# New order lists for all five engines of a fused attention and FFN kernel, with TensorE's identity products as entries of the list

## The chip, the cores and the metric

The kernel runs on one core of a Trainium2 chip. The metric is the device time of one execution in microseconds (us). Before the change it is 241.96 us, the median of three runs (241.48 to 242.43). Five engines work side by side: TensorE (PE in the profile; PEld are its weight loads), VectorE (DVE), ScalarE (ACT), GpSimd (POOL) and SyncE (SP, which here only issues transfers). Each works its own instructions strictly in the order in which they stand, and waits at an instruction until the semaphores of its inputs have been raised.

## The reference

Four batches of eight heads, 768 positions of 64 values. A small 8x8 matrix per head is normalised five times over rows and columns and mixes the eight blocks of 96 positions of K and V. Attention is then local: block i of Q against block i of the mixed K and V. Its output, 3072 tokens of 512 values, goes through an FFN with a leaky rectifier whose slope differs by column.

```python
k_sorted = np.einsum('bhij,bhjcd->bhicd', P, k_b).reshape(B, H, S, D)
v_sorted = np.einsum('bhij,bhjcd->bhicd', P, v_b).reshape(B, H, S, D)
...
scores = scale * np.matmul(q_b, k_sb.transpose(0, 1, 2, 4, 3))
scores = scores - np.max(scores, axis=-1, keepdims=True)
attn = np.exp(scores)
attn = attn / (np.sum(attn, axis=-1, keepdims=True) + 1e-09)
return np.matmul(attn, v_sb).reshape(B, H, S, D).astype(np.float32)
...
h = x @ w_in
g = np.maximum(h, 0.0) + alpha * np.minimum(h, 0.0)
return (g @ w_out).astype(np.float32)
```

## The kernel before

**Stages.** Each batch's K, V and Q are loaded, mixed and laid out, and then attention and the FFN run through the tokens, with the next batch's preparation between them. A *group* g is one block of one batch: g0 to g7 are batch 0, g8 to g15 batch 1, up to g31. A *chunk* c is what one round of the FFN's first product takes: c0 is g0 and g1, c1 is g2 and g3 (192 tokens each), c2 to c8 are four groups each (384 tokens). An *output tile* t is 128 tokens, t0 to t23.

- *K and V of batches 1 to 3.* POOL copies the loaded K (`KS`) into a zero-padded layout `KSz` (`conv_k`, line 672), and V (`VST`) into `VDz` (`conv_v`, line 715; all copies that either engine can make are recorded at line 428, the helper `copy`). Eight products with a mixing matrix (`BDM` or `BDV`) turn a part into PSUM (lines 685 and 726), and ScalarE or VectorE copies it on to `KT` or `VS` (line 428). `KSz` has three places and `VDz` four, so a copy waits until TensorE has read the part that stood there. `conv_v` of batch 0 goes from `VST` into a free part of `hT`, its products are at line 731.
- *Q of batches 1 to 3.* POOL issues eight transfers into `QN` (line 457), then SP issues six transposing transfers `QN` to `QTz` (line 465).
- *Attention of a group.* Scores (lines 769 and 772) into `psS`, their maximum on VectorE (line 778). In batch 0 the scores are computed a second time, turned, with the maximum subtracted (lines 784 and 793), and ScalarE takes the exponential (`ET`, line 816). From batch 1 on ScalarE takes eight exponentials (`Esb`, line 805), and SP issues a transposing transfer `Esb` to `ET` (line 810). Then come the products with V (line 825, `psO`), the reciprocal of the sums (line 833), the scaled result `xq` (line 836), its transposition on TensorE (line 851) or, from batch 2 on, by SP (line 844), and the copy to `xT` (line 428).
- *FFN.* For each of 16 parts of a chunk four products with `w_in` (line 875) into one of two banks `psH` (for c0 also the bank `psP`), ScalarE's rectified copy `t` (line 885) and VectorE's result `hT` (line 888). The bank is free when VectorE is done. An output tile is four quarters of four products with `w_out` each (line 914), a copy to one of four stages `outstg` (line 428) and a store that SP issues (line 928). `hT` holds two chunks of 384 tokens.

**Order.** Nothing is scheduled on the chip. The program adds operations with their inputs and outputs to a graph, numbered 0 to 1225 in the order in which the code adds them. The table `SEQ` lists these numbers in one order for all engines, and `arrange` walks it: each entry goes to the end of its engine's list. Where an operation can run on several engines, a letter says which: `a` ScalarE, `d` VectorE, `p` POOL; without one it is the first of those named in the code. `emit` then writes each list out with the waits that the graph asks for. The planned durations in the graph matter for the entries' start times in the plan, which `fill` and `idle` read.

**Identity products.** `warm` makes products of the identity matrix with 512 columns (line 1041), whose result nobody reads. `fill` puts them into the planned gaps of TensorE's list ahead of the first `w_in` product and of the first `w_out` product; `idle` puts them into planned gaps of 300 ns and more after that, in a bank that is free. There are 55: 15, 8, 2, 2, 4, 2, 5, 5, 1 and 3 ahead of the first `w_in` product, and 1, 1, 1, 2, 1, 1 and 1 behind it.

Of the kernel before, what the change touches and what calls it, by code (L numbers as in the profile page):

```python
# [7 lines left out]
AP = bass.AP  # L8
# [24 lines left out]
0 2 11 3 7 4 8 1 22 9 14 42 28 43 44 19 45 46 5 47 18 48 49 15 50 51 39 52 53 6 54 55 56 25 57 58 29 59 60 61  # L33
23 62 63 12 64 65 66 132 89 37 67 83 68 81 31 69 84 70 32 87 71 13 10 91 88 85 72 40 73 74 90 130 75 76 86 41
77 133 78 82 79 131 92 80 93 134 138 102 94d 103a 26 104 147 95 105a 100 148 98 96d 97 108 99a 38 101d 109d
158 159 118 106a 119d 107a 35 114 160 149 36 115d 116 16 120 117a 112a 146 150 111 110d 113d 161 30 17 122 27
135 123a 24 121a 128 144 124 129d 126 143 125a 151 127d 21 145 136 152 137 162 153 163 164 154 183 155 165
166a 34 156 184 20 157a 167 141 192 33 185 168 193 140 169 194 142 186 170 201 195 139 247 246 249 248 253 252
171 202 198 196 203 204 199 197 187 219 200 220 205 216 213 217 214 218 206 221 215 228 207 188 225 189 222
272 226 229 227 223 230 234 224 260 235 237 236 261 190 262 250 191a 238 269 208 309 270 231 251a 209 239 174  # L40
210 402 401 232 233 240 211 257 254 271 263 212d 255a 290 256 310d 278 264 258 291 273 346 259a 265 266 304
312d 292 279 267 280 303 241 268 293 284 242 281 243 301 282 337 347a 283 274 300 338 302a 244 299 287 245d
285 339 286 311 351d 294 340 313 295 305 296 275 314 288 315 289 319 276a 177 297 306d 316 320 321 307 317 378
298a 318 178 325 308a 379 322 341 323 348 342 182 380 326 324 354 349a 327 328 343 352 180 329 331 353d 381
344 350 345d 356 179 332 330 382 357a 334 383 333 372 335 181 359a 336 360 384 363 361 387 364 362 418 393 403
388a 385 365 366 419 369 358 367 373 370 368 420 374 386d 355d 428 371 394d 391 421 429 434 390d 444 431 392a
435 389 395 432 375 430 436 446 396d 452 445 376d 397 433 404 449 453 437 398a 454 464 447 458 465 399 459 455
474 176 400a 460 405 448 175 456 173 450 466 406 478 451d 422 457 475 476 482 172 423 467 504 424 461 483 494
484 505 462 425 407 477a 463 414 495 426a 480 485 572 573 408a 481d 438 409 486 548 412 439 496 487 508 506
277 440 491 479 417 534 410 411 509 413 416 535 415 507d 441 488 492 497 442d 524 493 489 510 490 515 511a 377  # L50
525 512 516 549 517 513 526 514 468 536 518 537d 521 469 470 519 527 560 520 538 471 561 539a 542 522 472d 571
543 523 498 540 562 550 499 570 500 541d 501 545 544 502a 563 574 546 554 575d 596 547 555 605 557 556 606a
611 503 578 558 576 551 559 579 427 612 580 581 552a 597 584 577 582 533 590 583 585 598 586 528 443 587 529
530 609 613 636 531 599 614 625 532d 608 591 610a 626 588 569 607 592 589 627 637 564 615 616 473 565 634 566
619 635a 628 567 617 638 568d 593 639a 618 620 640 622 641a 621 645 600 594a 676 643 601 658 623 595 677 642
661 659 624 644 678 662 602 663 660 670 679 703 671 603 704 664 604a 647 667 705 665d 648 629 666 691 630 631
692 713 672 668 706 669 712 738 685 739 715 673 686 693 714 687 674 740 675 632 716 633d 688 717 718 697 719d
752 689 741 767 698 690 680 751 749 699 700 553 649 750d 720 701 646 694 702 721 777 722 723 695a 768 753 696
726 780 754a 681 732 682 724 748 727 725 683 733 769 747 728 734 707 729 708 770 709 755 730 742 731 756 778
710 802 779a 812 757 758 782 776 759 761 760 781 735 762 783a 763 657 764 803 736a 813 651 784 814d 849 787  # L60
785 743 765 786 788 653 804 744 654 789 766 745 852 771 793 772 773 805 846 815 794 837 796 816a 795 811 774
790 797 656 798 817 799 853 818a 791d 819 800 838 650 825 820 847 801 839 826 821 655 822 848 806 850 840 807
831 808 652 851a 872 832 883 827 792 823 833 880 824 854 881a 886 834 855 828 856 835 836 884 860 910 885a
829d 857 861 873 882 711 866 858 862 874 887 867 859 911 908 863 909d 888 875 864 841 865 889 900 912 684 890
891 913a 842 901 894 892 746 868 893 902 869 843 844 876 870d 914 897 895 877 896 919 903 898 915d 916 878 934
917 920 879 935 980 918 936 809 981 899 928 775 925 929 904 830 930 926 921 927 960 737 931 961 922 932 937
905 962 906 942 933 982 907 945 923a 963 986 946 948 987 943 949 944 988 938 950 939 940 954 947 989 1006 955
957 1007 810 983 958 1008 959 951 956 971 952d 964 968 972 1009 984a 973 1017 969 965 845 1032 970 977 966 974
941 978 990 979 975 1018 985 976 997 1033 994 924 998 1019 999 995 967 996 1003 991 1000 1004 1020 1005 1001
1034 1002 1023 992 1014 993 1010 1046 1011 1015 1012 1024 1047 1035 1016 1058 1025 1026 871 1059 1029 1027  # L70
1013 1048 1028 1030 1060 1031 1040 1021d 1043 1078 1041 1061 1036 1044 1079 1037 1042 1022 1084 1045 1052 1085
953 1049 1053 1086 1054 1080 1038 1055 1050d 1066 1056 1087 1062 1067 1115 1063 1068 1104 1057 1072 1064 1069
1105 1065 1116 1070 1071 1106 1117 1075 1088 1118 1076 1107 1089 1073 1077 1081 1074 1039 1095 1090 1082a 1092
1096 1051 1136 1097 1093 1119a 1094 1101 1091 1108 1102 1098 1120 1103 1137 1099 1109 1100 1121 1083 1110 1112
1122 1111 1160 1123 1113 1114 1127 1124 1128 1138 1129 1125 1126 1133 1130 1134 1161 1135 1131 1132 1145 1142
1146 1162 1147 1143 1144 1139 1148 1163 1149 1140a 1150 1151 1141 1154 1152 1181 1153 1155 1156 1157 1166 1158
1202 1159 1167 1168 1182 1172 1169 1173 1208 1174 1170 1171 1178 1175 1179 1183 1180 1176 1177 1190 1187 1191
1184 1192 1188 1189 1196 1185a 1193 1186 1197 1209 1198 1194 1195 1210 1164d 1199 1165 1203 1200 1201 1204
1220 1211 1205 1212d 1221 1213 1206d 1222 1223 1207 1214 1224 1215 1216 1225 1217 1218 1219
# [41 lines left out]
class _Graph:  # L121
# [79 lines left out]
    def arrange(self, table):  # L201
        assert len(table) == len(self.ops)
        letters = {"p": "pool", "a": "act", "d": "dve"}
        free = dict.fromkeys(ENGS, 0.0)
        free["pool"] = 400.0
        loads = [0.0, 0.0, {"n": 2, "mark": 193, "usable": 0.0, "end": 0.0, "fills": True}]
        self.order = {e: [] for e in ENGS}
        done = set()
        for x in table:
            op = self.ops[int(x.rstrip("pad"))]  # L210
            e = letters.get(x[-1], op.engs[0])
            assert e in op.engs and op.deps <= done
            done.add(op.idx)
            at = max(free[e], self.ready_at(op, e))
            op.eng, op.start, op.pos = e, at, len(self.order[e])
            free[e], op.end = self.span(op, e, at, free, loads)
            self.order[e].append(op)
        return max(op.end for op in self.ops)

    def fill(self, make, unit, first, spans):  # L220

        out, last = [], self.ops[first].end + 300
        for op in self.order["pe"]:
            for lo, hi in spans:
                begin = max(last, lo)
                n = int((op.start - begin) * 0.9 / unit)
                if op.start <= hi and n > 0:
                    x = _Op("pe", lambda e, n=n: make(e, n), n * unit, 0.0, None, len(self.ops))
                    x.start, x.end, x.banks = begin, begin + n * unit, set()
                    x.deps.add(first)  # L230
                    self.ops.append(x)
                    out.append(x)
            out.append(op)
            last = max(last, op.end)
        for pos, op in enumerate(out):
            op.pos = pos
        self.order["pe"] = out

    def idle(self, make, unit, banks, lo, hi, least):

        used = {k: sorted((op for op in self.ops if k in op.banks), key=lambda o: o.start) for k in banks}
        out, last = [], 0.0
        for op in self.order["pe"]:
            n = int((op.start - last) * 0.85 / unit)
# [841 lines left out]
```

## Time and profile before

| | us |
|---|---|
| median of three runs | 241.96 |
| profiled execution | 242.12 |
| its span, from the first to the last instruction | 240.1 |
| TensorE busy, with the identity products | 231.3 |
| VectorE busy | 172.4 |
| ScalarE busy | 153.9 |
| POOL busy | 99.8 |
| granted TensorE clock, as a share of full speed | 1.0 |

The rows of the profile are to be read so: a group of instructions gives line, engine, operation, what it writes and reads and in which shape, the count, and behind the bar the busy time, the mean duration in ns, the idle time of the engine ahead of them, and what ended that idle time. The timeline and the chain of waits give the start in the span, the duration and what ran. The chain is followed back from the last instruction, at each step to what released it. Matmuls are pipelined and the profile models their ends, so that the duration of a short group is longer than the distance to the next start. SP's and POOL's issues of transfers have a duration of their own, and a time to landing.

### The profile page before, as it was taken

The numbers are of one execution on the slowest core, as the hardware profiler recorded it, in microseconds if no ns is written. First come the engines' busy times: TensorE is split into PE (matmuls) and PEld (weight loads), VectorE is DVE, ScalarE is ACT, GpSimd is POOL, SyncE is SP. The second block draws the span as 40 slices with busy tenths as digits, with TensorE's granted clock in tenths as the row PEclk, the third lists the DMA queues.
The fourth block names the chain that finished last, engine by engine and source line by source line (L and its number), as shares of the span: only waits on it lengthen the run. The fifth ranks groups of instructions, "written<-read, shape, count | busy, mean of one in ns | idle before, by whom it ended". The sixth has DMA issues, their size and how long they took to land.

```text
span 240.1 us, 6229 instructions
## 1 busy us (share of the span) xinstructions
PE 231.3 (96%) x2519; PEld 142.3 (59%) x2519; DVE 172.4 (72%) x348; ACT 153.9 (64%) x422; POOL 99.8 (42%) x146
## 2 busy tenths in 40 slices
PE   7889998999999999999999999999999999999995
PEld 3446676688566656655666566555655555555554
DVE  4756887998989888777958677756777666645542
ACT  4576466678978788977667778567756655444510
POOL 7989707924689964518859841000000000000000
PEclk9999999999999999999999999999999999999999
DMA  5999999999967999999749974593745426101023
GB/s 101 205 211 217 155 220 197 176 180 166 161 118 141 144 128 163 161 180 164 153 101 69 114 137 79 111 183 64 141 121 112 123 49 177 39 0 44 0 91 131
DMA packets 71981, 31.36 MB, mean 131 GB/s; under 512 B 64512, under 2 KB 67344, under 8 KB 71952
## 3 DMA queue, kind: packets, MB, share of 16 engines
q0 software_dynamic: 23408, 13.63, 42.6%
q1 hardware_dynamic: 48544, 17.33, 35.2%
q8 instruction: 20, 0.33, 0.6%
q14 instruction: 9, 0.07, 0.1%
HBM read 27.28 MB, written 6.29 MB: 140 GB/s over the span
## 4 chain that ended last, share of the span: by engine, by line
PE 71%; POOL 11%; DMA 10%; DVE 5%; issue 1%; ACT 0%; POOLq 0%
PE psH L875 29%; PE psYP L914 27%; DMA KS<-in_k_dram 10%; POOL VDz L428 5%; PE psS L914 4%; PE psO L825 3%; PE psS L769 3%; PE psYP L726 2%; PE psYP L685 2%; DVE hT L888 1%; POOL KSz L672 1%; POOL w_in_bf L959 1%; POOL VDz L512 1%; DVE VDz L428 1%; PE psO L914 1%
## 5 line engine op out<-in xcount | busy, mean ns | idle before, releaser
L875 PE MATMUL psH<-xT,w_in_bf 128*128 128x384 bf16 (+1 forms) x556 | 98.4, 311 | 0.6 <-DVE hT L888 0.4
L888 DVE SCALAR_TENSOR_TENSOR hT<-t,omaT,psH 128x384 bf16<-128x384 f32 (+1 forms) x139 | 77.7, 571 | 29.2 <-ACT t L885 27.5
L885 ACT ACTIVATE t<-psH 128x384 f32<-128x384 f32 (+1 forms) x139 | 62.7, 461 | 50.5 <-PE psH L875 49.2
L914 PE MATMUL psYP<-w_out_bf,hT 128*128 128x512 bf16 x336 | 82.9, 379 | 0.0
L875 PEld LDWEIGHTS psH<-xT,w_in_bf 128*128 128x128 bf16 x556 | 49.0, 98 | 29.2 <-DVE hT L888 4.1
L914 PEld LDWEIGHTS psYP<-w_out_bf,hT 128*128 128x128 bf16 x336 | 31.1, 98 | 30.3 <-DVE outstg L428 0.6
L805 ACT ACTIVATE Esb<-psS,nf 96x96 bf16<-96x96 f32 x192 | 46.2, 344 | 2.0 <-DVE nf L778 1.8
L428 POOL COPY VDz<-VST 64x384 bf16<-64x384 bf16 x40 | 34.1, 853 | 15.6 <-PE psYP L726 12.8
L672 POOL COPY KSz<-KS 64x512 bf16<-64x512 bf16 x36 | 22.0, 612 | 18.8 <-PE psYP L685 8.8
L778 DVE TENSOR_REDUCE nf<-psS 96x8 f32<-96x768 f32 x24 | 22.8, 948 | 5.5 <-PE psS L769 5.1
L836 DVE TENSOR_TENSOR xq<-psO,rec 96x512 bf16<-96x512 f32 x31 | 21.2, 683 | 0.6
L457 POOL DMA_DIRECT2D QN<-in_q_dram x24 | 19.9, 837 | 0.3 <-POOL QN L517 0.3
L1041 PE MATMUL psYP<-identb 128*128 128x512 bf16 x51 | 15.1, 417 | 0.7 <-ACT identb L428 0.7
L825 PEld LDWEIGHTS psO<-VS,ET 112*128 112x128 bf16 x248 | 11.3, 98 | 4.7 <-DVE xT L428 0.7
L769 PEld LDWEIGHTS psS<-KT,QTz 128*96 128x96 bf16 x192 | 11.9, 125 | 2.5
L833 DVE RECIPROCAL rec<-psO 96x8 f32<-96x8 f32 x31 | 6.2, 200 | 9.8 <-PE psO L825 9.8
L825 PE MATMUL psO<-VS,ET 112*128 112x65 bf16 x248 | 12.7, 194 | 0.4 <-DVE xT L428 0.3
L769 PE MATMUL psS<-KT,QTz 128*96 128x96 bf16 x192 | 12.6, 209 | 0.0
L428 ACT ACTIVATE VS<-psYP 112x512 bf16<-112x512 f32 x15 | 10.3, 686 | 3.1 <-PE psYP L726 2.6
L428 ACT ACTIVATE KT<-psYP 128x512 bf16<-128x512 f32 x15 | 8.9, 596 | 3.8 <-PE psYP L685 2.5
L726 PEld LDWEIGHTS psYP<-BDV,VDz 128*128 128x128 bf16 x192 | 8.0, 98 | 3.6 <-POOL VDz L428 0.8
L726 PE MATMUL psYP<-BDV,VDz 128*128 128x64 bf16 x192 | 9.6, 193 | 0.5 <-POOL VDz L428 0.5
(142 smaller groups left out, 204.0 us busy)
## 6 DMA issues: line engine op xcount, KB each, us to landing
out_dram<-outstg SPq DMA_DIRECT2D x23, 256.0 KB, 2.6
KS<-in_k_dram POOLq DMA_DIRECT2D x3, 768.0 KB, 8.7
QN<-in_q_dram POOLq DMA_DIRECT2D x24, 96.0 KB, 3.8
w_in_bf<-in_moe_w_in_dram POOLq DMA_DIRECT2D x4, 512.0 KB, 11.9
w_out_bf<-in_moe_w_out_dram POOLq DMA_DIRECT2D x2, 1024.0 KB, 23.3
VST<-in_v_dram POOLq DMA_DIRECT2D x4, 384.0 KB, 18.3
hT<-in_q_dram POOLq DMA_DIRECT2D x1, 768.0 KB, 7.0
VST<-in_v_dram POOLq DMA_DIRECT2D x1, 768.0 KB, 10.9
```

The source lines that it names most:

```text
L428: return e.activation(o, i, ACTF.Copy) if e is nc.scalar else e.tensor_copy(o, i)
L672: G.add(POOL, lambda e, hp=hp: e.tensor_copy(AP(KSz, hp * 64 * 3072 + u % 3 * 1024 + hp * 64, [[3072, 64], [128, 8], [1, 64]]), AP(KS[n], ...
L726: inst = e.matmul(AP(t, off + dd * 64, [[row, 128], [1, 64]]), AP(VDz, (u % VSL * 8 + dd) * 128, [[VSL * 1024, 128], [1, 128]]), AP(BDV, b ...
L769: inst = e.matmul(o, AP(QTz[n], hp * 3072 + h4 * 768 + i * 96, [[6144, 128], [1, 96]]), AP(KT[n], (h4 * 8 + i) * bk, [[ld, 128], [64, 2], ...
L778: G.add(DVE, lambda e: e.tensor_reduce(AP(nx, 0, [[8, 96], [4, 2], [1, 4]]), AP(psX, 0, [[1024, 96], [512, 2], [96, 4], [1, 96]]), AxisLis ...
L805: inst = e.activation(AP(Esb[me], p * 128, [[1024, 96], [64, 2], [1, 48]]), AP(psX, (p // 4) * 512 + (p % 4) * 96, [[1024, 96], [48, 2], [ ...
L825: inst = e.matmul(AP(psZ, hp * 512 + h4 * 68, [[1024, 128], [1, 65]]), AP(ET[me] if far else ET[m], pos(h4, hp) * 96, [[800, nk], [1, 128] ...
L836: G.add(DVE, lambda e: e.tensor_tensor(out=AP(xq[me], 0, [[512, 96], [256, 2], [64, 4], [1, 64]]), in0=AP(psZ, 0, [[1024, 96], [512, 2], [ ...
L875: inst = e.matmul(AP(pt, poff, [[1024, 128], [1, n]]), AP(w_in_bf, kt * DFF + ft * 128, [[KT_TILES * DFF, 128], [1, 128]]), AP(xT, kt * XR ...
L885: G.add(ACT, lambda e: e.activation(AP(t1[tb], 0, [[384, 128], [1, n]]), AP(pt, poff, [[1024, 128], [1, n]]), ACTF.Relu, scale=-1.0), t_ac ...
L888: G.add(DVE, lambda e: e.scalar_tensor_tensor(out=AP(hT, ft * RING + tok % RING, [[FT_TILES * RING, 128], [1, n]]), in0=AP(t1[tb], 0, [[38 ...
L914: inst = e.matmul(AP(bank[0], bank[1], [[1024, 128], [1, n]]), AP(hT, ft * RING + tok % RING, [[FT_TILES * RING, 128], [1, 128]]), AP(w_ou ...
```

## The change

The table is another one; it was searched anew from batch 0's k on. The code outside it changes in these points.

- The identity products are entries of the table, such as `i3Y`: three products into bank `Y`. `filler` adds them when `arrange` comes to them, behind the identity matrix and behind the readers of what last stood in that bank. `fill` and `idle` are gone. There are 46 products in 11 entries: 15, 8, 2, 2, 4, 1, 3, 3, 3, 3 and 2, all ahead of the first `w_in` product.
- Three kinds of operations may run on more engines: the copies of batch 0's Q, `conv_v` of batch 0 and the padding of `KT`. Q's copies and the padding stay where they were.
- 45 copies change their engine: 20 go from ScalarE to VectorE, 20 from VectorE to ScalarE, and three to and two from POOL (all five are `conv_v` of batch 0).

What changes in the order, where the prediction speaks of it:

- POOL: of batch 0's `conv_v` it takes parts 0, 4 and 7 (before: 2 and 5). The load of batch 2's V is issued ahead of the first `KSz` copy. The eight issues of batch 2's Q (line 457) stand behind all sixteen V copies of batch 2; they stood among the last of them.
- VectorE: g0's `xT` copy stands behind g2's maximum. The maxima of g3 to g7 stand ahead of more of c0's and c1's `hT` results. The two `VDz` copies that stood ahead of and behind g5's maximum go to ScalarE and to a place behind g6's `xq`.
- TensorE: c0's first product stands behind g2's second scores. The third quarter of t1 stands behind c2's first product, the product of V part 4 of batch 1 ahead of it.
- SP: the stores of t1 and t0 stand ahead of g8's transposition of `Esb`; they stood behind g10's and g11's. Three of the six transpositions of batch 1's Q stand behind it; all six stood ahead of it.
- The last four products, their copy and their store stand where they stood; ahead of them the quarters of the last three output tiles are in another order.

```diff
 SEQ = """
-0 2 11 3 7 4 8 1 22 9 14 42 28 43 44 19 45 46 5 47 18 48 49 15 50 51 39 52 53 6 54 55 56 25 57 58 29 59 60 61
...
+0 2 11 7 3 4 1 8 9 i15Y 22 42 28 14 43 44 45 46 19 47 18 48 5 49 50 51 15 39 52 53 54 6 55 56 57 25 58 29 59
...
 """.split()
...
-    def arrange(self, table):
-        assert len(table) == len(self.ops)
+    def filler(self, x, used, make, unit, first):
+        n, bank = int(x[1:-1]), x[-1]
+        written, free = used.get(bank, (False, []))
+        assert not written or free
+        op = _Op(("pe",), lambda e: make(e, n, bank), n * unit, 0.0, None, len(self.ops))
+        op.banks, op.deps = set(), {first, *free}
+        self.ops.append(op)
+        return op
+
+    def arrange(self, table, names, make, unit, first):
+        assert sum(x[0] != "i" for x in table) == len(self.ops)
...
-        loads = [0.0, 0.0, {"n": 2, "mark": 193, "usable": 0.0, "end": 0.0, "fills": True}]
+        loads = [0.0, 0.0, {"n": 2, "mark": 193, "usable": 0.0, "end": 0.0, "fills": False}]
...
-            op = self.ops[int(x.rstrip("pad"))]
-            e = letters.get(x[-1], op.engs[0])
+            if x[0] == "i":
+                op = self.filler(x, used, make, unit, first)
+                e = "pe"
+            else:
+                op = self.ops[int(x.rstrip("pad"))]
+                e = letters.get(x[-1], op.engs[0])
             assert e in op.engs and op.deps <= done
             done.add(op.idx)
+            for k in op.banks:
+                k = names.get(k, k)
+                used[k] = (True, [] if e == "pe" else used[k][1] + [op.idx])
...
-    def fill(self, make, unit, first, spans):
...
-    def idle(self, make, unit, banks, lo, hi, least):
...
-        G.add(ACT, lambda e: copy(e, o, i), t_act(512), r=keys, w=[("Q0", u)], prio=prio)
+        G.add(EITHER, lambda e: copy(e, o, i), t_either(512), r=keys, w=[("Q0", u)], prio=prio)
...
-            G.add(POOL if u % 3 == 2 else EITHER, lambda e: copy(e, o, i), {"act": 858, "dve": 540, "pool": 860},
+            G.add(ANY, lambda e: copy(e, o, i), {"act": 858, "dve": 540, "pool": 860},
                   r=vst, w=[("VD", u)], prio=prio)
...
-    G.fill(warm, 215, ident_op, [(5000, first_y[0].start), (ffn_ops[0].start + 1, ffn_ops[1].start)])
-    G.idle(warm, 215, {"psY": (psYP, 0), ("psP", 0): (psYP, 512), ("psH", 0): (psH, 0), ("psH", 1): (psH, 512),
-                       "psO0": (psO, 0), "psO1": (psO, 512)}, first_y[0].start, 84e3, 300)
+    total = G.arrange(SEQ, {k: x[0] for k, x in banks.items()}, warm, 215, ident_op)
```

More of the change, by code (lines that the diff above doesn't have):

```diff
@@ L218, in arrange @@
         return max(op.end for op in self.ops)
-    def fill(self, make, unit, first, spans):
[L222 to L237, printed above, removed]
-    def idle(self, make, unit, banks, lo, hi, least):
[L241 to L244, printed above, removed]
-            if lo <= last and op.start <= hi and op.start - last >= least and n > 0:
-                for k, bank in banks.items():
-                    before = [u for u in used[k] if u.start < last]
-                    after = [u for u in used[k] if u.start >= last]
-                    free = [u for u in before if u.eng != "pe" and u.end + 46 > last]
-                    if not before or before[-1].eng == "pe" or free or not after or after[0].eng != "pe":
-                        continue
-                    x = _Op("pe", lambda e, n=n, bank=bank: make(e, n, bank), n * unit, 0.0, None, len(self.ops))
-                    x.start, x.end, x.banks = last, last + n * unit, {k}
-                    while before and before[-1].eng != "pe":
-                        x.deps.add(before.pop().idx)
-                    self.ops.append(x)
-                    out.append(x)
-                    break
-            out.append(op)
-            last = max(last, op.end)
-        for pos, op in enumerate(out):
-            op.pos = pos
-        self.order["pe"] = out
     def emit(self, nc, sems):
```

100 lines of the change are left out of this document (48 added, 52 removed), and 9 rows, old and new, of the table SEQ.

## The prediction

> **What bounds the kernel now.** I read the page's first part, then the busy times by stage, then the groups, then the chain where TensorE still waits. The stages are cut at the first `w_in` product (28.66 us), the first `w_in` product of chunk c2 (61.28), TensorE's last wait for POOL in batch 2's V (78.46) and the first product of c4 (113.72). A stage's columns are its bounds and length, then busy time and instructions of TensorE, its weight loads, VectorE, ScalarE and POOL.
>
> ```profile
> span 240.1 us, 6229 instructions
> PE 231.3 (96%) x2519; PEld 142.3 (59%) x2519; DVE 172.4 (72%) x348; ACT 153.9 (64%) x422; POOL 99.8 (42%) x146
> ...
> 0.00:28.66 28.66, 25.06 (x575) 14.90 (x575) 19.01 (x64) 16.42 (x32) 25.44 (x43) 1.00 0.94 178
> 28.66:61.28 32.62, 31.22 (x459) 24.38 (x460) 28.69 (x67) 22.62 (x57) 14.93 (x22) 1.00 1.32 188
> 61.28:78.46 17.18, 16.71 (x187) 10.35 (x186) 15.66 (x30) 13.96 (x44) 14.84 (x19) 1.00 0.79 135
> 78.46:113.72 35.26, 34.68 (x353) 21.33 (x354) 27.44 (x49) 28.30 (x88) 21.07 (x31) 1.00 1.12 159
> 113.72:240.06 126.34, 123.63 (x954) 71.39 (x950) 81.55 (x141) 72.59 (x204) 23.51 (x33) 1.00 0.51 97
> ```
>
> The same with the identity products alone (line L1041; the later stages have none):
>
> ```profile
> 0.00:28.66 28.66, 13.38 (x47) 4.34 (x47) 1.00 0.94 178
> 28.66:61.28 32.62, 2.12 (x6) 0.58 (x6) 1.00 1.32 188
> 61.28:78.46 17.18, 0.76 (x2) 0.20 (x2) 1.00 0.79 135
> ```
>
> TensorE is 96% busy, but that counts the identity products and the modelled ends of short groups. Time is to be won only where TensorE does no product that the result needs. The last stage has 2.71 us of idle time, most of it the tail behind the last product. Ahead of it lie 0.58 idle (78 to 114), 0.47 idle + 0.76 identity (61 to 78), 1.40 idle + 2.12 identity (29 to 61) and 3.60 idle + 13.38 identity before the first FFN product. From 28.66 to 61.28 VectorE is busy for 28.69 of 32.62 us; from there to 78.46 it has 15.66 and POOL 14.84 of 17.18. The chain of waits names the same two engines, VectorE around 42 us and POOL around 74:
>
> ```profile
> 41.11 0.97 DVE VDz L428
> 42.10 0.95 DVE nm L778
> ...
> 43.53 0.90 DVE VDz L428
> ...
> 73.69 0.84 POOL QN L457
> ...
> 75.86 0.77 POOL QN L457
> ```
>
> **The change part by part.** (A) *Up to the first FFN product.* The lists are the same through batch 0's k. Of the eight V copies (`conv_v`) POOL takes three, ScalarE three and VectorE two; it was two, three and three. The masks `mkj` and `mkjV` come earlier; g0's `xT` copy goes from ScalarE to VectorE, behind g2's maximum. There is one identity product fewer (46 for 47).
>
> ```profile
> L428 DVE CAST VS<-psO 112x512 bf16<-112x512 f32 x3 | 2.0, 688 | 1.4 <-PE psO L731 1.4
> L778 DVE TENSOR_REDUCE nm<-psS 96x8 bf16<-96x768 f32 x7 | 6.6, 948 | 0.0
> ```
>
> VectorE waited 1.4 us for V products here, so at most that is won. The maximum of 0.948 put ahead of `xT` is what can be lost. I take a gain of 0.2, about the middle of the bounds -0.9 and +1.4.
>
> (B) *From there to c2's first product.* What moves between the engines, priced by the groups (second number behind the bar: mean ns of one):
>
> ```profile
> L428 DVE COPY VDz<-VST 64x384 bf16<-64x384 bf16 x6 | 4.2, 718 | 0.2
> L428 DVE COPY xT<-psO 128x384 bf16<-128x384 bf16 x9 | 3.2, 351 | 1.6 <-PE psO L851 1.6
> L428 DVE CAST KT<-psYP 128x512 bf16<-128x512 f32 x4 | 2.7, 685 | 1.0 <-PE psYP L685 1.0
> L428 DVE CAST VS<-psYP 112x512 bf16<-112x512 f32 x11 | 7.6, 689 | 2.1 <-PE psYP L726 1.7 <-PE psYP L731 0.4
> L428 DVE COPY outstg<-psYP 128x512 f32<-128x512 f32 x9 | 6.2, 687 | 1.0 <-PE psYP L914 0.6 <-DMA out_dram<-outstg 0.3
> L778 DVE TENSOR_REDUCE nf<-psS 96x8 f32<-96x768 f32 x24 | 22.8, 948 | 5.5 <-PE psS L769 5.1
> ...
> 30.50 0.22 DVE L631 TENSOR_TENSOR BDM<-mkhM,dsel 128x64 bf16<-128x64 f32 x1
> ...
> 33.52 0.73 DVE L888 SCALAR_TENSOR_TENSOR hT<-t,omaT,psH 128x192 bf16<-128x192 f32 x2
> ```
>
> Ahead of c2's first product VectorE loses two `xT` copies, one VDz, one KT and one VS copy and g8's maximum: 2 x 0.351 + 0.718 + 0.685 + 0.689 + 0.948 = 3.74. It gains two `xT` copies, one VDz, one outstg and one VS copy (2.80) and two small mask products at the 0.22 of the like one at 30.50: 3.24. So it has 0.5 less to do. ScalarE, idle for 10.0 us of this stage, takes the rest. The order counts for more. Of the two VDz copies in the chain above, the first goes to ScalarE and the second stands far later. Between g2's and g5's maximum VectorE's list held 14 results `hT`, one VDz and one `xT` copy beside the rest; now it holds 12 results and two `xT` copies. Two results at 0.365 (half of 0.73) and the copy of 0.97 go, 0.35 comes: 1.35 less ahead of g5's maximum, which began at 42.10, and attention hangs on it. For the whole stage I count the 0.5 and a third of VectorE's 3.93 idle (1.3): c2's first product comes 1.8 us earlier. But a quarter of an output tile (L914, four products) is put behind that point, and one V product (L726) ahead of it. Half of the 1.73 below and the distance of the next two starts give 0.86 - 0.23 = 0.6:
>
> ```profile
> 59.72 1.73 PE psYP L914 x8
> ...
> 70.56 0.40 PE L726 MATMUL psYP<-BDV,VDz 128*128 128x64 bf16 x8
> 70.79 0.49 PE L875 MATMUL psH<-xT,w_in_bf 128*128 128x384 bf16 x2
> ```
>
> Net 1.2. Bounds: 0 (the waits only change place) and 3.93 + 0.5 - 0.6 = 3.8 (no wait is left). For the six identity products that go I add nothing: they filled waits.
>
> VectorE's VDz copy took 0.97 at 41.11, beside POOL's copy of 40.88, and 0.60 at 60.61, after POOL's copies of that time:
>
> ```profile
> 40.88 0.82 POOL L428 COPY VDz<-VST 64x384 bf16<-64x384 bf16 x1
> ...
> 60.61 0.60 DVE L428 COPY VDz<-VST 64x384 bf16<-64x384 bf16 x1
> ```
>
> The Trainium skill ("Advanced Engine Details and Errata", VectorE Performance Modes) says that VectorE's second port is shared with GpSimd, so that the two block each other; the rows agree. By that rule alone the four such copies that VectorE keeps of six would cost 4 x 0.97 = 3.9, undisturbed 2.4, by the group's mean 2.9.
>
> (C) *61.28 to 78.46.* POOL's V copies for batch 2 set the pace:
>
> ```profile
> 62.39 1.00 POOL L428 COPY VDz<-VST 64x384 bf16<-64x384 bf16 x1 [1.57 <-PE psYP L726]
> ...
> 78.46 0.41 PE L726 MATMUL psYP<-BDV,VDz 128*128 128x64 bf16 x8 [0.47 <-POOL VDz L428]
> ```
>
> The issues of batch 2's q move behind all sixteen V copies. So POOL is rid of two of them on the way to the copy awaited at 78.46: 0.84 + 0.77 = 1.6 of the 16 us since 62.39. The 14 V copies on that way stay, and TensorE comes earlier too, so a wait may stay. The two identity products (2 x 0.216, by the 1.73 for eight) go: 0.4, bounds -0.5 (a wait twice as long) and +0.9 (0.47 and 0.43).
>
> (D) *78.46 to 113.72.* Idle 0.58, and short groups may hide as much. The order is new throughout: 0.4, bounds -1.0 and +1.0. (E) *The rest.* The last four products, their copy and the store stand as they stood:
>
> ```profile
> 237.40 0.38 ACT L428 ACTIVATE outstg<-psS 128x256 f32<-128x256 f32 x1 [6.46 <-PE psS L914]
> ```
>
> Nothing, bounds -0.8 and +0.4. Sum: 0.2 + 1.2 + 0.4 + 0.4 = 2.2 of the span of 240.1, so 237.9. The profiled execution took 242.12, 2.0 around its span: 239.9. The median of the runs, 241.96, is 0.16 lower: **239.7**.
>
> **The rivals.** *Other waits, the same time: 241.6.* Every engine works its list in order; what VectorE gives up may be lost again at the next bank or landing. Against it speaks the count ahead of g5's maximum, for it that the count ends there, with a third of the stage gone. Then A and C leave 0.4.
>
> *The transposition queue: 243.8.* SP issues one after the other. The stores of output tiles 1 and 0 now stand ahead of g8's E transposition (L810), and tile 1's waits for its copy on VectorE. Landing times are those of L810, then of L465:
>
> ```profile
> 64.85 0.68 DVE L428 COPY outstg<-psYP 128x512 f32<-128x512 f32 x1
> ...
> 70.31 0.41 PE L825 MATMUL psO<-VS,ET 112*128 112x65 bf16 x8
> ...
> 74.31 0.86 SPq L928 DMA_DIRECT2D out_dram<-outstg  x2
> ...
> DMA to landing us min/median/max: 2.8/3.0/7.2
> ...
> DMA to landing us min/median/max: 3.0/4.0/8.9
> ```
>
> The copy ends at 65.53 - 1.8 = 63.7 and two issues take 0.86: the transposition starts at 64.6 and lands at 67.6 with the median. TensorE's product with it is due at 70.31 - 1.8 = 68.5 and doesn't wait. With 7.2 of flight it waits 3.3, with 8.9 it waits 5.0; with the middle, 4.1, the time is 239.7 + 4.1 = 243.8. It costs from a flight of 3.9 on and makes the kernel slower from 7.5. For it: the flight of 7.2 is in the page, and the list's first outputs stood behind it so far. Against: three of the six q transpositions ahead of it are now behind it.
>
> *The clock falls: 241.4.* The identity products keep TensorE at work.
>
> ```profile
> 2.79 4.92 PE L1041 MATMUL psYP<-identb 128*128 128x512 bf16 x15 [0.72 <-ACT identb L428]
> ...
> 38.23 0.40 PE L685 MATMUL psYP<-BDM,KSz 128*128 128x64 bf16 x8 [0.92 <-POOL KSz L672]
> ```
>
> The first 15 took 0.33 each where 0.216 is usual: 15 x 0.112 = 1.7 us for one warming. The longest idle time behind it, 0.92, cost nothing. The Trainium skill ("TensorE: Matmul & The Clock Gate", Part 1: The HAM clock gate) halves the clock after an idle window of about 3.4 us; by that rule it takes a hole that no row here shows.
>
> **How the numbers follow.** Forecast 0.64, other waits 0.19, transposition queue 0.14, clock 0.03. 0.5% (1.2 us) is what runs of this kernel can tell from no change. Faster is the forecast, 0.64; the same are other waits and clock, 0.22; slower is the queue, 0.14. The forecast's own range is 237.3 (B near its upper bound) to 240.7. The range takes in other waits and clock and part of the queue: **237.3 to 242.6**.
>
> **What would show it.** g5's maximum (L778) begins ahead of 41 us, and c2's first product (L875, 384 columns) at 59 to 60; the wait of L726 for POOL after 60 us stays under 0.5; L825 waits for no transposition of g8; the stage from c4's first product on lasts as long. It is wrong if VectorE's idle time between the two first products stays near 3.9, or if TensorE waits for landings in ET or `xT`.

## The result and the profile after

| | before | after |
|---|---|---|
| median of 19 runs, us | 241.99 | 240.34 |
| ratio, 95% interval | 1 | 0.994 (0.9925 to 0.9956) |
| profiled execution, us | 242.12 | 240.34 |
| its span, us | 240.1 | 238.6 |

The kernel became 1.65 us faster, where 2.2 was forecast. The time lies inside the range, but it was not reached in the forecast way: three of the five stages ended about 1 us or more away from their term, and the errors nearly cancel. That is luck, and the range says little: 237.3 to 242.6 also holds the time of the kernel before. Some executions of these kernels fell in a slower state with a lower clock, and the medians of the experiments leave them out.

The busy times by stage show this. The cuts are the landmarks of the prediction: first `w_in` product, first `w_in` product of c2, the product of batch 2's V part 4, first product of c4. The columns are those of the prediction's table. 29 matmul records are missing in this trace (2481 of 2510, the weight loads are all there), all of them products with `w_out`: 13 from 35 us up to c4's first product and 16 behind it. So the busy TensorE of all stages but the first is too low; their bounds are not touched by that.

```profile
span 238.6 us, 6176 instructions
...
0.00:29.42 29.42, 26.36 (x590) 15.68 (x591) 18.87 (x66) 16.37 (x31) 26.49 (x44) 1.00 0.96 180
29.42:58.78 29.36, 28.12 (x441) 23.39 (x442) 25.72 (x63) 22.85 (x55) 14.48 (x22) 1.00 1.33 183
58.78:76.10 17.32, 16.13 (x170) 9.89 (x170) 15.30 (x27) 14.54 (x46) 15.78 (x20) 1.00 0.89 156
76.10:110.58 34.48, 34.16 (x361) 21.89 (x365) 29.35 (x54) 27.73 (x88) 20.10 (x30) 1.00 1.13 161
110.58:238.60 128.02, 122.81 (x933) 71.58 (x947) 80.36 (x141) 72.73 (x205) 24.17 (x34) 1.00 0.56 97
```

Against the prediction's table the stages are 0.76 longer (29.42 for 28.66), 3.26 shorter, 0.14 longer, 0.78 shorter and 1.68 longer: c4's first product comes 3.14 us earlier, and more than half of that is gone at the end. TensorE's waits say where. Of the groups in the page, these two have a wait of a kind that the page of before does not have (behind the bar: busy time, mean of one, idle time ahead and what ended it):

```profile
L847 PE MATMUL psH<-xT,w_in_bf 128*128 128x384 bf16 (+1 forms) x556 | 97.2, 310 | 1.7 <-DVE VS L400 1.7
...
L797 PE MATMUL psO<-VS,ET 112*128 112x65 bf16 x248 | 12.7, 194 | 1.0 <-DMA ET<-Esb 1.0
```

*The wait of 1.0 is g8's E.* These are SP's rows of the timeline, then the landing times that the view of a line gives for the two stores alone and for this transposition alone, then TensorE's row:

```profile
63.25 0.85 SPq L900 DMA_DIRECT2D out_dram<-outstg  x2
64.15 2.58 SPq L782 DMA_TRANSPOSE ET<-Esb  x1
...
DMA to landing us min/median/max: 4.3/5.2/6.0
...
DMA to landing us min/median/max: 6.3/6.3/6.3
...
70.48 0.42 PE L797 MATMUL psO<-VS,ET 112*128 112x65 bf16 x8 [1.03 <-DMA ET<-Esb]
```

The stores land at 67.5 and 69.7 and the transposition issued behind them at 64.15 + 6.3 = 70.4, so its *flight*, the time from issue to landing, is 6.3. The product starts at once.

*The wait of 1.7 is g19's x*, ahead of c5's first product at 137.56, although the page names a copy to `VS`:

```profile
129.61 0.58 SPq L900 DMA_DIRECT2D out_dram<-outstg  x1
130.30 1.84 SPq L816 DMA_TRANSPOSE xT<-xq  x1
...
DMA to landing us min/median/max: 7.2/7.2/7.2
...
135.98 0.64 DVE L400 CAST VS<-psYP 112x512 bf16<-112x512 f32 x1
...
137.56 0.65 PE L847 MATMUL psH<-xT,w_in_bf 128*128 128x384 bf16 x3 [1.68 <-DVE VS L400]
```

The copy ended at 136.62, almost a microsecond ahead of the product. The transposition of x, which the product needs too, was issued at 130.30 and landed 7.2 later, at 137.5. Where the engine that the profile names had been done, look for a landing.

The 24 q loads of three batches fly longer too: the median is 3.8 us before and 5.7 after.

### The profile page after: what moved, and what is told of

The parts are those of the page before. It is cut to its first block, busy times and chain, and to the rows that moved or that the text cites. A ratio compares the mean times of both kernels' runs of the same rounds, so it can differ in the third digit from the quotient of the medians.

```text
span 238.6 us, 6176 instructions
## 1 busy us (share of the span) xinstructions
PE 227.6 (95%) x2481; PEld 142.4 (60%) x2510; DVE 169.6 (71%) x347; ACT 154.2 (65%) x422; POOL 101.0 (42%) x147
## 4 chain that ended last, share of the span: by engine, by line
PE 79%; DMA 7%; DVE 5%; ACT 4%; issue 2%; POOL 2%; POOLq 0%
PE psH L847 31%; PE psYP L886 28%; DMA VST<-in_v_dram 5%; PE psS L886 4%; PE psS L741 3%; PE psO L797 3%; DMA ET<-Esb 3%; PE psYP L698 2%; DVE hT L860 2%; PE psYP L657 1%; PE psS L756 1%; PE psO L823 1%; DVE nm L750 1%; ACT t L857 1%; DVE xq L808 1%
## 5 line engine op out<-in xcount | busy, mean ns | idle before, releaser
L847 PE MATMUL psH<-xT,w_in_bf 128*128 128x384 bf16 (+1 forms) x556 | 97.2, 310 | 1.7 <-DVE VS L400 1.7
L886 PE MATMUL psYP<-w_out_bf,hT 128*128 128x512 bf16 x307 | 77.5, 379 | 1.6 <-issue 0.2
L847 PEld LDWEIGHTS psH<-xT,w_in_bf 128*128 128x128 bf16 x556 | 50.0, 98 | 32.6 <-DVE hT L860 2.8
L1017 PE MATMUL psYP<-identb 128*128 128x512 bf16 x43 | 13.0, 442 | 0.7 <-ACT identb L400 0.7
L400 ACT ACTIVATE outstg<-psYP 128x512 f32<-128x512 f32 x12 | 7.0, 595 | 4.7 <-PE psYP L886 4.6
```

What stands on the lines that cost most here:

```text
L400: return e.activation(o, i, ACTF.Copy) if e is nc.scalar else e.tensor_copy(o, i)
L847: inst = e.matmul(AP(pt, poff, [[1024, 128], [1, n]]), AP(w_in_bf, kt * DFF + ft * 128, [[KT_TILES * DFF, 128], [1, 128]]), AP(xT, kt * XR ...
L886: inst = e.matmul(AP(bank[0], bank[1], [[1024, 128], [1, n]]), AP(hT, ft * RING + tok % RING, [[FT_TILES * RING, 128], [1, 128]]), AP(w_ou ...
```

## The experiments

All times are medians; the ratios are to the kernel before, run on the same chip. The changed kernel's ratio is 0.994. The order lies in the table alone, so each edit moves just the entries shown; the numbers in the diffs are entries. Where an edit makes the table a row longer, the line numbers in the trace are one higher.

**no_late_id.** The calls that put identity products behind the first `w_in` product are cut short:

```diff
-    G.fill(warm, 215, ident_op, [(5000, first_y[0].start), (ffn_ops[0].start + 1, ffn_ops[1].start)])
+    G.fill(warm, 215, ident_op, [(5000, first_y[0].start)])
...
-                       "psO0": (psO, 0), "psO1": (psO, 512)}, first_y[0].start, 84e3, 300)
+                       "psO0": (psO, 0), "psO1": (psO, 512)}, first_y[0].start, ffn_ops[0].start, 300)
```

> The kernel before without its eight identity products behind the first w_in product; nothing else differs. Theory (the new order is what gains; these products mostly filled waits): 0.4 us off for the two that stood in front of batch 2's V, nothing for the other six, so 241.6 (bounds 241.2 to 242.0), and the first product of c4 at 113.3 instead of 113.7. Rival (leaving out identity products is the gain): all eight cost 0.216 each, 1.7 us in all, so 240.3, as fast as the changed kernel.

241.89 us, ratio 1.0007 (0.9988 to 1.0026). The rival is out: the eight products, which it priced at 1.7 us, are worth nothing. c4's first product came 0.27 earlier, which a later wait of 0.7 us for an output copy on VectorE took back. Not even the 0.4 of term C is there.

**stores_back** and **x_first**, the two landings. 277 and 377 are the stores of t0 and t1 (467 is g10's E transposition, 497 g11's), 696 the store of t6, 774 g19's x transposition:

```diff
 stores_back
-398 452 435 377 432 444 399 277 453 404 433
+398 452 435 432 444 399 453 404 433
...
-463 408 467 482
+463 408 467 277 482
...
-440 492 497 534
+440 492 497 377 534
 x_first
-786 772 696 813 773 848 796 814 873 655 774 799
+786 772 813 773 848 796 814 873 655 774 696 799
```

> The changed kernel with the stores of output tiles 0 and 1 back behind the E transpositions of g10 and g11 on SP; nothing else differs. Theory (TensorE's wait of 1.4 us for g8's E at 70.4 is time lost to the two stores ahead of it in SP's queue): g8's transposition is issued as before at about 64 and lands ahead of 69.5, the wait goes, and 1.0 us of it reaches the end unless a later landing takes it: 239.3, c4's first product at about 109.4. Rival (the wait is hidden behind what VectorE and POOL still owe): under 0.3 us, 240.1 to 240.5, with a wait of the same size at one of the next products.

239.24 us, ratio 0.9889 (0.9865 to 0.9912): 1.1 us off (0.5% of the time), as the theory said. g8's E was issued at 62.73, landed 5.2 later, and the wait is gone. Ahead of c5 TensorE waited 0.7. So the two stores cost more than their own way through the queue. The transposition landed 2.5 earlier, at 67.9 for 70.4: 1.1 of it is the flight, 1.4 the issue. In the changed kernel g8's exponentials ended at 62.35, but SP stood at the stores until the copy to `outstg` ended at 63.23, and then issued the two for 0.85:

```profile
60.42 1.93 ACT L777 ACTIVATE Esb<-psS,nf 96x96 bf16<-96x96 f32 x8
...
62.55 0.68 DVE L400 COPY outstg<-psYP 128x512 f32<-128x512 f32 x1
```

> The changed kernel with the store of output tile 6 behind g19's x transposition on SP; nothing else differs. Theory (TensorE's 2 us without work ahead of c5's first product are a wait for that transposition, which is in flight from 130.3 to 137.5 with the store and batch 3's q loads beside it): without the store ahead of it it lands 0.7 to 1.5 us earlier and so does the end: 238.9 to 239.6. Rival 1 (the q loads alone make the flight long): under 0.3 us. Rival 2 (VectorE's copy to VS, which the profile names as the one that was waited for, is what holds c5's first product up): nothing, 240.3.

239.11 us, ratio 0.9888 (0.9859 to 0.9917): 1.2 us off, in the upper half of what the theory gave. The copy to `VS` is as it was, so rival 2 is out. This landing row is that of g19's x transposition in x_first, issued at 130.3 like the one of the changed kernel:

```profile
DMA to landing us min/median/max: 6.3/6.3/6.3
```

It lands 0.8 earlier, at 136.65 for 137.46, and TensorE's wait is 0.86 for 1.68. The rest of the flight has another cause.

**x_first_q_later** asks whether it is POOL's loads: two issues of batch 3's q (652 and 655) go behind four `KSz` copies.

```diff
-873 655 774 696 799 791 797 815 652 825
+873 774 696 799 791 797 815 825
...
-820 822 849 821
+820 822 849 655 652 821
```

> x_first (the store of output tile 6 behind g19's x transposition) with, in addition, the issues of two parts of batch 3's q (2 and 5) on POOL behind four KSz copies, some 3 us later. Theory (loads in flight beside a transposition make its flight long, as the store did): g19's x transposition, 6.3 in flight in x_first, takes 4 to 5, lands at 134.3 to 135.3, and TensorE's wait ahead of c5 (0.9 in x_first) goes: 238.2 to 238.7, unless the q transpositions, which come 1 to 3 later, are waited for. Rival (only what stands ahead of it in SP's queue counts, not POOL's loads): it lands at 136.6 as in x_first and the time stays at 239.1.

The same row of this kernel (issued at 131.46):

```profile
DMA to landing us min/median/max: 4.0/4.0/4.0
```

The flight fell from 6.3 to 4.0, and the landing came 1.2 earlier (135.5) although the issue came 1.2 later. That the wait ahead of c5 is gone proves nothing here: c5's first product started at 136.87, behind the landing of x_first too. all_in_new, below, is the better witness. The time did not move: 239.48 us, ratio 0.9886 (0.9856 to 0.9916), the same as x_first. In the profiled execution TensorE was already about 1.0 us behind that of x_first at c2's first product (59.9 for 58.9), where the two kernels don't differ; so large a spread of the beginning hides an effect of 0.9.

**tail_before** and **both_fixes**: the rest from c4's first product on (entry 697) is that of before, without and with the two stores put back.

> The changed kernel's order and engines up to c4's first product, and the order and engines of the kernel before for all that is left from there. Theory (up to c4's first product the change gains 3.2 us, and the new order behind it loses 1.7 of them at one landing): c4's first product stays at about 110.4, the old rest lasts 126.3 as it did or up to 1 us more where its own transfers now meet TensorE earlier: 238.6 to 239.8. Rival (what the head gains is only moved, since the same transfers bound the rest in either order): the rest becomes longer by as much as in the changed kernel, 240.3.

239.45 us, ratio 0.99 (0.9873 to 0.9927), the theory's. The last stage, and the landing of g19's x in it (issued at 129.80):

```profile
111.11:237.50 126.39, 123.69 (x949) 71.55 (x947) 81.33 (x141) 72.80 (x205) 25.56 (x36) 1.00 0.54 99
...
DMA to landing us min/median/max: 3.9/3.9/3.9
```

126.39 long, as before (126.34), for 128.02 in the changed kernel: what the head won is kept. The old order has no store ahead of this transposition and one q load in flight at its issue (the changed kernel has four), and it lands at 133.7, 1.5 us ahead of c5's first product.

> The order and engines of the changed kernel up to c4's first product, those of the kernel before from there, and the stores of output tiles 0 and 1 behind the E transpositions of g10 and g11. Theory (the wait for g8's E and the one for g19's x are separate losses): what stores_back took off, 0.5 to 1.1 us, comes off tail_before's 239.45 too: 238.3 to 239.0, c4's first product at 109.9 to 110.4. Rival (one and the same 1.1 us, taken off at either place): 239.2 to 239.5.

238.12 us, ratio 0.9856 (0.981 to 0.9903): this version beats both kernels, the changed one by 0.8% (0.9856/0.994). The median is the theory's, but the interval reaches into the rival's range. The trace decides: TensorE waits neither at g8's E nor ahead of c5, and at 140 us the kernel is 4.1 us ahead of the one before, where the changed kernel is 1.3 ahead (the table of progress below). So the two waits are separate losses. **all_in_new**, the changed kernel with the three edits above, comes to nearly the same:

> The changed kernel with all three edits: the stores of tiles 0 and 1 behind the E transpositions of g10 and g11, the store of tile 6 behind g19's x, two of batch 3's q loads 3 us later. Theory (two separate landings): the gains add, 1.1 and 1.2 to 1.9: 237.3 to 238.2, as fast as both_fixes or faster. Rival (taking the wait at 70 away only makes TensorE wait longer at c5, as stores_back already showed for 0.7 us): 238.4 to 239.1.

238.43 us, ratio 0.9861 (0.9825 to 0.9896). That is 1.9 us under the changed kernel; the theory's 237.3 to 238.2 was a little too much, the rival's 238.4 its lower end, and the interval takes in both. That the waits are separate rests on the traces. This one also shows what lengthened the flight of g19's x. stores_back issued it at 129.78, with the store ahead of it and the loads where they were, and it landed at 135.93; all_in_new issued it at 129.72 and it landed at 134.49, 0.6 ahead of c5's first product. The store alone was worth 0.8 in x_first, so that some 0.6 is left for the two loads, an estimate from single executions.

**vdz_back**: one VDz copy (310) back to VectorE ahead of g5's maximum (291):

```diff
-233 211 291 263
+233 211 310d 291 263
...
-280 339 310 295
+280 339 295
```

> The changed kernel with one VDz copy (batch 1's part 0, second half) from ScalarE back to VectorE, straight ahead of g5's maximum, about where it stood before. Theory (the count of VectorE's work ahead of that maximum sets c1's attention and c2's first product): the maximum begins 0.97 later, at 40.4, c2's first product 0.6 to 1.0 later, at 59.4 to 59.8; of that 0.3 to 1.0 us reaches the end, less what g8's E transposition is waited for less: 240.6 to 241.3. Rival (the maximum is early enough in either place, and the gain up to c2 has another cause): c2's first product stays at 58.8 and the time at 240.3.

VectorE's and TensorE's rows of the timeline, of the changed kernel:

```profile
39.47 0.95 DVE L750 TENSOR_REDUCE nm<-psS 96x8 bf16<-96x768 f32 x1
...
58.78 1.48 PE L847 MATMUL psH<-xT,w_in_bf 128*128 128x384 bf16 x8
```

and of vdz_back:

```profile
39.68 0.53 DVE L400 COPY VDz<-VST 64x384 bf16<-64x384 bf16 x1
40.23 0.95 DVE L750 TENSOR_REDUCE nm<-psS 96x8 bf16<-96x768 f32 x1
...
59.54 1.15 PE L847 MATMUL psH<-xT,w_in_bf 128*128 128x384 bf16 x6
```

The maximum is 0.76 later and c2's first product is 0.76 later: what stands ahead of g5's maximum on VectorE moves that product one for one. How much of it reaches the end is not settled: 241.13 us, ratio 0.9966 (0.9936 to 0.9996), overlaps with 0.994. In the profile (span 238.3, the fastest of the twelve executions) it is gone, since TensorE waits 0.7 at g8's E and 1.0 at c5, for 1.0 and 1.7.

**head_to_c2** and **rest_from_c2** split the change at c2's first product (entry 428).

> The order and engines of the changed kernel up to c2's first product, those of the kernel before for all that is left from there (with the third quarter of t1 behind that product, and without the late identity products). Theory (the gain is made by VectorE's order ahead of c2's first product): that product at 58.8 to 59.2 and the rest as before behind it, plus 0.6 for the quarter that is put off: 1.3 to 1.8 us off, 240.2 to 240.7, if g8's E, which now is issued behind fewer q transpositions, is there at 68. Rival (the rest is bound by POOL's V copies and the transpositions, whose times do not move with TensorE): c3's first product at 86.5 or later and the time at 241.3 to 241.9.

242.00 us, ratio 0.9994 (0.9976 to 1.0013): near the rival's number, but not for its reason. c3's first product came at 87.27 (before: 87.36). ScalarE's row of before, then ScalarE's and TensorE's rows of head_to_c2:

```profile
60.11 1.93 ACT L805 ACTIVATE Esb<-psS,nf 96x96 bf16<-96x96 f32 x8
...
60.28 1.94 ACT L778 ACTIVATE Esb<-psS,nf 96x96 bf16<-96x96 f32 x8 [0.57 <-DVE nf L751]
...
62.27 0.56 PE L742 MATMUL psS<-KT,QTz 128*96 128x96 bf16 x8 [1.46 <-ACT Esb L778]
```

c2's first product is nearly as early as in the changed kernel (59.12 for 58.78), but g8's exponentials are no earlier than before (60.28 for 60.11). The old order puts g9's scores next, which need the bank that these exponentials free. All that the head won is lost in this one wait. In the changed kernel c2's second part, two quarters of t1 and two V parts stand ahead of those scores.

> The other way round than head_to_c2: the order and engines of the kernel before up to c2's first product (without the late identity products), those of the changed kernel for all that is left from there. Theory (up to c2 the new order does 1.7 us more work, but it needs the new order behind c2 to keep it; behind c2 the new order alone wins what TensorE waited for POOL at 78, some 0.8 to 1.1 us, and since TensorE comes later to the landings of g8's E and g19's x these cost it less): 240.6 to 241.3. Rival 1 (all of the gain comes from behind c2): 240.0 to 240.4. Rival 2 (neither half gains without the other): 241.6 to 242.0.

242.80 us, ratio 1.0027 (1.0007 to 1.0047): rival 2, and a little worse. The stretch from 74 to 90 won 1 us here too (the table of progress below), and the wait ahead of c5 took more: it is 1.49, with g19's x issued 2 us later than in the changed kernel and 7.0 in flight. My theory took this landing for a fixed time to which a later TensorE loses less. It isn't: the issue follows TensorE's own work, and the store and the loads beside it follow too.

**qn_behind** and **qn_back** test the reason of term C. 410 to 417 are batch 2's q issues, 535 the last V copy:

```diff
 qn_behind (on no_late_id)
-463 414 495 ... 548 412 439 ... 479 417 534 410 411 509 413 416 535 415
+463 495 ... 548 439 ... 479 534 509 535 414 412 417 410 411 413 416 415
 qn_back (on the changed kernel)
-424 494 508 463
+424 494 414 412 508 463
...
-525 512 516 414 468 517 513 536 412 549
+525 512 516 468 517 513 536 549
```

> The kernel no_late_id (the one before without the eight late identity products; 241.9) with the eight issues of batch 2's q on POOL moved behind all sixteen V copies of batch 2, as in the changed kernel; nothing else differs. Theory (POOL's V copies set the pace there, and two issues of 0.84 and 0.77 stand on their way): TensorE's wait of 0.8 us for POOL ahead of V part 4 goes, c3's first product comes 0.4 to 0.8 earlier, 241.2 to 241.5. Rival (a V copy waits for its place in VDz, which TensorE sets free): under 0.2, 241.8.

242.15 us, ratio 1.001 (0.9988 to 1.0032), no gain. V part 4 came 0.9 earlier than in no_late_id and waited for nothing, but POOL's next work is late now:

```profile
79.23 6.58 POOL L457 DMA_DIRECT2D QN<-in_q_dram  x8
85.75 1.36 POOL L672 COPY KSz<-KS 64x512 bf16<-64x512 bf16 x2
...
87.25 0.39 PE L685 MATMUL psYP<-BDM,KSz 128*128 128x64 bf16 x8 [1.11 <-POOL KSz L672]
```

> The changed kernel with two of the eight issues of batch 2's q (parts 4 and 2) back among POOL's V copies, ahead of the fourteenth-last step to V part 4, as before; the other six stay behind all of them. Theory (moving these issues is what rids TensorE of its wait for POOL at 78): V part 4's product waits 0.8 to 1.6 for POOL again, c3's first product comes 0.5 to 1.3 later than 84.4; of it 0.3 to 1.0 reaches the end, since g19's x lands no later than now: 240.6 to 241.3. Rival (the slack of POOL is larger than two issues, since the order of the copies changed as well): under 0.2, 240.3.

247.33 us, ratio 1.0225 (1.019 to 1.026), far more than either theory. POOL's, then TensorE's row:

```profile
76.73 1.66 POOL L429 DMA_DIRECT2D QN<-in_q_dram  x2 [4.66 <-DMA QTz<-QN]
...
82.61 0.61 PE L698 MATMUL psYP<-BDV,VDz 128*128 128x64 bf16 x8 [4.79 <-POOL VDz L400]
```

A q load overwrites `QN`, so it waits until batch 1's transpositions from `QN` have landed. The change put three of them behind g8's E on SP; a load issued earlier stands before them with all of POOL behind it. So the move of the q issues is no gain of its own: the new order of SP forces it. The wait of 4.79 is not the whole loss. TensorE's clock was at half speed for the 5.9 us of work behind it (last section), which costs some 2.9 us, an estimate; the profiled execution, 248.89, is the slowest of the six.

## Why the prediction was right, and where it was not

The forecast of a faster kernel came true, but both signs that were to prove it wrong showed up: VectorE's idle time between the two first products stayed near 3.9 (3.64), and TensorE waited for landings in `ET` (1.03) and `xT` (1.68). g5's maximum and c2's first product came as early as foreseen or earlier, and TensorE's wait for POOL is gone.

| term | predicted | in the profile |
|---|---|---|
| A, to the first `w_in` product | 0.2 | -0.76 |
| B, to c2's first product (1.2 and the 0.6 put off) | 1.8 | 3.26 |
| C, to V part 4 (0.4 less the 0.6) | -0.2 | -0.14 |
| D, to c4's first product | 0.4 | 0.78 |
| E, the rest | 0 | -1.68 |
| sum | 2.2 | 1.46 |

*E failed, and outside its bounds (-0.8 to +0.4).* "The last four products, their copy and the store stand as they stood" looked only at the end of the stage. Its order is new from 110 on too, and in it a store went ahead of g19's x transposition. tail_before shows that the old order of this stage loses nothing. This is the rival of the transposition queue at a place that I had not looked at; at the place that I had named it took 1.0 more. There the issue was foreseen well (64.6, it came at 64.15) and so was the need (68.5, TensorE stood there at 69.4). What was wrong is the flight: I took the median of 3.0 as likely and put 0.14 on a wait. Yet the two longest flights that I had quoted, 7.2 and 8.9, are of this very place: in the kernel before they are g8's E, issued at 62.06, and the q transposition ahead of it, issued at 59.77, both beside a load of 768 KB that landed at 67.56.

*B's place was right, its size too small, and one of its tests failed.* g5's maximum began at 39.47 (ahead of 41), 2.6 us earlier than before where the count gave 1.35, and vdz_back shows that it sets c2's first product. But VectorE's idle time in this stage is 29.36 - 25.72 = 3.64, near the 3.93 that I had said would prove the step wrong. The third of it that I counted on was not what was won: VectorE is busy for 28.69 - 25.72 = 3.0 us less in this stage, not 0.5. Half of that is no gain: four small mask instructions, 1.5 us, now stand ahead of the first `w_in` product, which the new order puts later. The VDz copies make another 1.2 (four in 3.2 us before, three in 2.0 after). Stage D has more to do (29.35 for 27.44). c2's first product at 58.78 for 59 to 60 is therefore an early landmark more than progress. To measure progress, each product that is not an identity product can be priced by the lower quartile of the distance to the next start, by shape, in the trace of before (199.9 us in all), and added up until a given time; products whose records are missing are counted by their weight loads. The figures are good to about 0.2. By how much each kernel is ahead of the one before, in us:

| at us | changed | head_to_c2 | rest_from_c2 | both_fixes |
|---|---|---|---|---|
| 46 | 0.2 | -0.1 | 0.0 | 0.0 |
| 60 | 1.8 | 1.5 | 0.2 | 1.6 |
| 68 | 2.2 | 0.0 | -0.1 | 2.0 |
| 74 | 0.9 | -0.2 | -0.2 | 2.0 |
| 90 | 2.7 | 0.0 | 0.8 | 3.8 |
| 135 | 3.0 | 0.0 | 1.0 | 4.1 |
| 140 | 1.3 | 0.2 | -0.5 | 4.1 |

The changed kernel is 1.8 ahead at 60 (B said 1.2), loses 1.3 at g8's E, wins 1.8 by 90 and loses 1.7 at g19's x. A won nothing and lost nothing by 46; its -0.76 is a landmark that the new order put later.

*C held in size, not in its reasons.* Its -0.14 contains the 1.0 lost at g8's E, so the rest of it won more than was said. TensorE no longer waits for POOL at V part 4, as foreseen. The two identity products are worth nothing (no_late_id), and ridding POOL of two issues only moves the wait in the old order (qn_behind); together with the rest of the new order it is kept. *D* lies within its bounds.

*The other rivals.* Other waits at the same time, 241.6, is what head_to_c2 did: the gain of one stage went to the next bank. (The 0.4 that A and C were to leave there should have been 0.2 + 0.4 = 0.6, 241.4.) The clock did not fall in the changed kernel: 1.00 in every stage, with the longest wait 1.68. The four VDz copies that VectorE kept took 2.6 us, where I had 2.4 undisturbed and 3.9 disturbed: one ran beside a copy on POOL and took 0.98, the other three 0.53 each. The row of 0.60 at 60.61 that I read as undisturbed was not quite so, since POOL's copy of 59.95 ended at 60.82.

## What to carry to other kernels

In a kernel whose order is a list, a stage that ends earlier has won nothing until the work behind it can use the time: follow the list past the landmark, up to the next bank or landing. Look at every transposition in a queue that also carries stores, all the way to the end of the kernel, and price its flight by a row with loads beside it, not by the median of all; ask first which place the longest flight in the page comes from. Stores that nobody waits for belong behind the transposition that TensorE waits for next: here two of them held up its issue until their own copy was done, and its landing besides. Moving three of them and two loads was worth another 1.9 us (0.8%), about as much as the whole new table.

## What the runs showed of the hardware

*Transfers on SP's queue landed one behind the other.* The two stores and g8's E landed at 67.5, 69.7 and 70.4 in the order of their issue; as far as the profile tells, so did all 85 transfers of SP in each trace of this case. The Trainium skill ("DMA: Bandwidth & Descriptors", Queues, rings and completion order) says that descriptors on a DMA engine are consumed in the order of the ring, and that the engine takes turns between the queues that have work. The rows agree. Loads that POOL issues, on another queue, seem to lengthen a flight too: g19's x took 7.2 us with a store ahead of it and four q loads in flight at its issue, 6.3 with the store behind it, and 4.8 in all_in_new and 4.0 in x_first_q_later, where two of the loads came later as well.

*A hole of 4.79 us cost the clock.* qn_back was built for another question; its windows from its wait on (the number behind the five engines is the granted clock):

```profile
77.45:82.70 5.25, 0.46 (x5) 0.09 (x3) 1.50 (x3) 0.74 (x2) 4.90 (x8) 0.90 0.77 75
82.70:86.00 3.30, 3.30 (x27) 2.29 (x28) 0.95 (x1) 1.65 (x3) 3.24 (x5) 0.50 0.09 9
86.00:90.00 4.00, 3.78 (x33) 2.41 (x33) 2.65 (x6) 2.63 (x11) 3.90 (x6) 0.68 1.73 109
90.00:96.00 6.00, 5.94 (x83) 4.15 (x83) 5.40 (x11) 5.20 (x16) 1.73 (x3) 1.00 0.80 100
```

Half speed for the 3.3 us behind the hole and full speed again ahead of 90. If the clock knows only 0.50 and 1.00, 0.90 over 5.25 us means 1.0 at half speed at the end of the hole, and 0.68 over 4 us means 2.6 more: 6.9 us in all, 5.9 of them from TensorE's restart at 82.61 on. By the Trainium skill ("TensorE: Matmul & The Clock Gate", Part 1: The HAM clock gate) the clock is halved after an idle window of about 3.4 us and given back after a busy window of as long, the windows running freely. The hole agrees: the clock fell some 3.9 us into it and came back 5.9 us behind the restart, between one window and two. Waits of up to 1.68 us left the clock at 1.00. In the same execution the clock was 0.72 between 18.5 and 24.7 us, where TensorE's longest wait was 0.9 us; no run here explains that.
